# One level of Strassen for the hidden product of six of nine tiles: seven half-block products in place of eight

## The chip, the cores and the metric

The kernel runs on one core of a Trainium2 chip. A core has TensorE (PE in the profile: matrix products, with its weight loads listed as PEld), VectorE (DVE), ScalarE (ACT), GpSimd (POOL) and SyncE (SP, whose queue issues the transfers), an on-chip memory (SBUF) of 128 partitions, a product memory (PSUM) of eight banks of 512 float32 a partition, and HBM behind the DMA engines. The metric is the device time of one execution in microseconds (us).

## The reference

Attention inside chunks of 64 tokens, then a wide layer with g = h cos h:

```python
q, k, v: (8, 8, 576, 64) float32        # batch, heads, sequence, head size
scores = scale * q_c @ k_c.T            # per chunk of 64 tokens
attn = softmax(scores)                  # max subtracted, sum + 1e-9
x = (attn @ v_c) laid out as (4608, 512)
h = x @ w_in                            # (4608, 512) @ (512, 2048)
g = h * np.cos(h)
out = g @ w_out                         # (4608, 2048) @ (2048, 512)
```

The weights arrive as 64-bit floats and are joined to float32 on the chip.

## The kernel before, in words

The 4608 tokens are nine tiles of 512 (t = 0 to 8); the 2048 hidden columns are 16 blocks of 128 (fc). Every float32 factor of the two large products is kept as a rounded high part and the low rest, and a product is three matmuls: high by high, high by low, low by high.

For one (t, fc), `hidden` (line 485) sums h into one PSUM bank: four chunks of the 512 rows of w_in, three matmuls each, 12 matmuls with 128x128 weights (w_in) over 512 moving columns (x, transposed). `activated` (496) then takes six operations in turns of ACT and DVE: the nearest whole turn (506, ACT), h minus that many turns (507, DVE), the sine (508, ACT), times h (509, DVE), the rounded part g_hi (510, ACT) and the rest g_lo (511, DVE). `project` (528) adds g times w_out into four PSUM banks `acc`, one for each 128 tokens (sub), three matmuls of 512 columns each; `finish` (555) copies a bank out after the tile's last block, on ACT for even sub and DVE for odd, and stores it. h has two PSUM banks in turn (`ps_h`), the two attention banks `a0` and `a1` are separate. All matmuls go through line 196, so the trace tells them apart by their tiles.

The first two tiles and the splitting of the weights run in an order that a planner works out (`placed`, `in_order`); it isn't touched. From the third tile on (line 872) the order is written out: for each (t, fc) the product h, the projection of the block three before it (`LAG`), then the six operations. Between them attention for the next tile is threaded in: at fc = 0 a burst of score matmuls (64x64) into the h banks and `a0`, `a1`; row maxima and differences on DVE; at fc = 2 the exponentials on ACT, which need another function table than the sine (ACT_TABLE_LOAD); row sums, quotients and 32 transposes of 32x256 on DVE, spread over the steps by the queue `soon`; at fc = 12 a second burst, weights times v, whose result is split into the high and low parts of x. `take` issues the next entries of a queue; `kept` holds each engine to program order. Loads go through SyncE's queue in program order as well.

The weights stay in SBUF: `w_in` and `w_out`, 16 rooms each, high and low parts side by side (`w_parts`). GpSimd works only in the first stage.

Of the kernel before, what the change touches and what calls it, by code (L numbers as in the profile page):

```python
# [21 lines left out]
P = 128  # L22
# [10 lines left out]

SCORES = 0
WEIGHTED = 12

# [125 lines left out]
def attention_then_cos_ffn(ctx: ExitStack, tc, qT, kT, v, w_in, w_out, out, wide):  # L162
# [51 lines left out]
    w_parts = {}  # L214

# [18 lines left out]
    def split_weight(name, fc, low):  # L234
# [34 lines left out]
        def high():  # L269
            o = SHIFT if name == "in" else 0  # L270
            parts = wts.tile([P, 2 * n + PAD], F32R, name=f"w_{name}{fc}")
            hi, lo = parts[:, o : o + n], parts[:, o + n : o + 2 * n]
            kept(nc.scalar.copy(out=hi, in_=w()))  # L273
            w_parts[name, fc] = (hi, lo)

# [70 lines left out]
    def scores(t, g, banks):  # L346

        for j in range(2):  # L350
            qt, kt = queries.pop((t, 2 * g + j))
            for c in range(NCH):
                pr, par = divmod(c, 2)
                cs, ps = slice(c * CH, (c + 1) * CH), slice(par * CH, (par + 1) * CH)
                o = (j * NPR + pr) * CH
                for h in range(2):
                    hs = slice(h * CH, (h + 1) * CH)
                    matmul(
                        banks[h][ps, o : o + CH], qt[hs, cs], kt[hs, cs], start=True, stop=True
                    )  # L360
        e = weights_of(t, g).rearrange("p a (r h) k -> p a r h k", h=2)
        found = []
        for h in range(2):
            sv = banks[h].rearrange("p (a r k) -> p a r k", a=2, k=CH)
            m = att.tile([P, 2, NPR], F32, name="m", bufs=4)

            def largest(m=m, sv=sv):
                kept(nc.vector.tensor_reduce(out=m, in_=sv, op=ALU.max, axis=AX.X))

            def below(m=m, sv=sv, h=h):  # L370
                mb = m.unsqueeze(3).broadcast_to([P, 2, NPR, CH])
                kept(nc.vector.tensor_tensor(e[:, :, :, h], sv, mb, op=ALU.subtract))

            found.extend((largest, below))
# [64 lines left out]
    def weighted(t, hps, banks):  # L439
# [4 lines left out]
        for j, hp in enumerate(hps):  # L444
            pts = probs.pop((t, hp))
            vt = values.pop((t, hp))
            for pr in range(NPR):
                for par in range(2):
                    ks = slice(par * CH, (par + 1) * CH)
                    o = (j * NPR + pr) * CH  # L450
                    for h in range(2):
# [4 lines left out]
                            start=True, stop=True,  # L456
                        )
        if (t, g) not in x_parts:
# [55 lines left out]
    def activate(t, fc, h):  # L514
# [10 lines left out]
        for queue in (full, soon, late):  # L525
            take(queue, len(queue))

    def project(s):
        t, fc = order[s]
        first = s == 0 or order[s - 1][0] != t  # L530
        last = s == len(order) - 1 or order[s + 1][0] != t
        g_hi, g_lo = g_parts.pop((t, fc))
        w_hi, w_lo = w_parts["out", fc]
        sums_out = []
        for sub in range(NSUB):
# [3 lines left out]
            ss = slice(sub * P, (sub + 1) * P)  # L539

            n = DM // 2 if s == len(order) - 1 and sub == NSUB - 1 else DM
            for a in range(0, DM, n):
                cs = slice(a, a + n)
                matmul(o[:, cs], g_hi[:, ss], w_hi[:, cs], start=first, stop=False)
                matmul(o[:, cs], g_hi[:, ss], w_lo[:, cs], start=False, stop=False)
                matmul(o[:, cs], g_lo[:, ss], w_hi[:, cs], start=False, stop=last and a + n == DM)
                if last:
                    sums_out.append(lambda sub=sub, o=o, cs=cs: finish(t, sub, o, fc == NFC - 1, cs))
        return sums_out
# [5 lines left out]
    def finish(t, sub, o, whole, cs):  # L555
        r0 = t * TOK + sub * P
        to = out[r0 : r0 + P, cs]
# [5 lines left out]
        elif t < NT - 1:  # L563
            os = out_room(sub)
        else:
            if sub % 2 == 0:
                acc["last"] = x_room(t + 1, F32)
            os = acc["last"][:, sub % 2, cs]
        o = o[:, cs]
# [8 lines left out]
    def resume():  # L578

        for sub in range(NSUB):  # L580
            os = acc["partial", sub] = out_room(sub)
            nc.sync.dma_start(out=os, in_=partial[sub])

# [20 lines left out]
    def burst(t, step):  # L604
# [3 lines left out]
        if step == SCORES:  # L608
# [3 lines left out]
        late.extend(first[:2] + second[:2] + first[2:] + second[2:])  # L612

    def prefetch(t):
        for hp in range(HP):
            load_qk(t, hp)
        for hp in range(2):
            load_v(t, hp)
# [71 lines left out]
    def early(t):  # L690
        s, e, z, q, w, p = {}, {}, {}, {}, {}, {}
        for hp in range(HP):
# [10 lines left out]
            e[hp] = piece(ACT, 0.6, lambda hp=hp: exponentials(t, hp), banks_free[which], table=AF.Exp)  # L703
# [169 lines left out]
    for s in range(STAGE, len(order) + LAG):  # L873
        if s < len(order):
            t, fc = order[s]
            h = hidden(t, fc)
            if t + 1 < NT:
                attend(t + 1, fc)
            if fc == WEIGHTED + 1 and t + 2 < NT:
                prefetch(t + 2)  # L880
# [3 lines left out]
        if s < len(order) and t + 1 < NT and fc in (SCORES, WEIGHTED):  # L884
            burst(t + 1, fc)
            through += 1
            full.extend(project(through))
        if s < len(order):
            activate(t, fc, h)
            if t + 1 < NT and fc == 2:  # L890
                exponentials(t + 1)
        take(full, len(full))

# [53 lines left out]
```

## Time and profile before

| | |
|---|---|
| median of 3 runs | 854.6 us (854.23 to 854.71) |
| the profiled execution | 854.07 us, of which its span 852.3 us |
| PE busy | 839.6 us, 99% of the span, 5795 matmuls |
| DVE busy | 554.1 us, 65% |
| ACT busy | 389.3 us, 46% |
| POOL busy | 6.8 us, 1% |
| DMA | 57.52 MB, mean 67 GB/s |
| granted TensorE clock | 0.998 of full speed |

The span is the part of the execution that the trace covers, from the first to the last instruction; the execution's own time lies 1.8 us above it. PE's busy time is the union of its matmuls, which overlap each other at their ends: their distance from start to start is what a matmul costs in a row of them.

### The profile page before, as it was taken

The numbers are of one execution on the slowest core, as the hardware profiler recorded it, in microseconds if no ns is written. First come the engines' busy times: TensorE is split into PE (matmuls) and PEld (weight loads), VectorE is DVE, ScalarE is ACT, GpSimd is POOL, SyncE is SP. The second block draws the span as 40 slices with busy tenths as digits, with TensorE's granted clock in tenths as the row PEclk, the third lists the DMA queues.
The fourth block names the chain that finished last, engine by engine and source line by source line (L and its number), as shares of the span: only waits on it lengthen the run. The fifth ranks groups of instructions, "written<-read, shape, count | busy, mean of one in ns | idle before, by whom it ended". The sixth has DMA issues, their size and how long they took to land.

```text
span 852.3 us, 14049 instructions
## 1 busy us (share of the span) xinstructions
PE 839.6 (99%) x5795; PEld 694.5 (81%) x5795; DVE 554.1 (65%) x942; ACT 389.3 (46%) x637; POOL 6.8 (1%) x12
## 2 busy tenths in 40 slices
PE   6999999999999999999999999999999999999998
PEld 5878888888888888888888888888888888888886
DVE  6978888744786458755775568646974577544332
ACT  4999973333433344342533353335333353333332
POOL 1010000000000000000000000000000000000000
PEclk9999999999999999999999999999999999999999
DMA  9990200420300211020302030022002020001001
GB/s 342 415 412 18 75 1 1 149 99 1 121 4 0 76 62 64 0 75 2 123 1 75 1 125 1 1 75 98 28 0 75 2 75 0 2 1 50 1 1 49
DMA packets 26704, 57.52 MB, mean 67 GB/s; under 512 B 2961, under 2 KB 3217, under 8 KB 26641
## 3 DMA queue, kind: packets, MB, share of 16 engines
q1 hardware_dynamic: 26640, 56.63, 18.3%
q8 instruction: 45, 0.74, 0.4%
q14 instruction: 19, 0.15, 0.1%
HBM read 46.14 MB, written 10.49 MB: 66 GB/s over the span
## 4 chain that ended last, share of the span: by engine, by line
PE 93%; ACT 4%; DVE 1%; DMA 1%; issue 0%; POOL 0%; SPq 0%; ACTq 0%; POOLq 0%
PE h L196 47%; PE acc L196 45%; PE a L196 2%; ACT half L265 1%; DMA kt<-in_kT_dram 1%; ACT w L263 0%; ACT x L469 0%; ACT w_out L273 0%; ACT L381 0%; ACT g_hi L510 0%; ACT g L508 0%; ACT e L381 0%; DVE x L472 0%; ACT w_in L273 0%; POOL e L401 0%
## 5 line engine op out<-in xcount | busy, mean ns | idle before, releaser
L196 PE MATMUL h<-x,w_in 128*128 128x512 f32 x1728 | 413.9, 390 | 0.2 <-DVE g L509 0.2
L196 PEld LDWEIGHTS h<-x,w_in 128*128 128x128 f32 x1728 | 323.8, 188 | 67.9 <-DVE g L509 0.6
L196 PE MATMUL acc<-w_out,g_hi 128*128 128x512 f32 x1154 | 356.9, 390 | 0.0
L196 PEld LDWEIGHTS acc<-w_out,g_hi 128*128 128x128 f32 x1154 | 215.3, 188 | 45.1
L196 PE MATMUL acc<-w_out,g_lo 128*128 128x512 f32 x577 | 224.4, 389 | 0.0
L507 DVE SCALAR_TENSOR_TENSOR g<-g,h 128x512 f32<-128x512 int32 x144 | 98.5, 684 | 141.3 <-ACT g L506 140.3
L506 ACT ACTIVATE g<-h 128x512 int32<-128x512 f32 x144 | 85.9, 597 | 198.8 <-PE h L196 198.6
L508 ACT ACTIVATE g<-g 128x512 f32<-128x512 f32 x144 | 91.1, 633 | 132.1 <-DVE g L507 132.0
L511 DVE TENSOR_TENSOR g_lo<-g,g_hi 128x512 fp32r<-128x512 f32 x144 | 99.6, 691 | 62.1 <-ACT g_hi L510 59.4
L509 DVE TENSOR_TENSOR g<-h,g 128x512 f32<-128x512 f32 x144 | 99.5, 691 | 61.4 <-ACT g L508 59.4
L510 ACT CAST g_hi<-g 128x512 fp32r<-128x512 f32 x144 | 89.5, 621 | 104.6 <-DVE g L509 96.5
L196 PEld LDWEIGHTS acc<-w_out,g_lo 128*128 128x128 f32 x577 | 108.3, 188 | 22.6
L431 DVE STREAM_TRANSPOSE pts<-e 32x256 f32<-32x256 f32 x128 | 55.5, 435 | 2.0
L431 DVE STREAM_TRANSPOSE e<-e 32x256 f32<-32x256 f32 x96 | 41.8, 435 | 1.8
L391 DVE TENSOR_REDUCE z<-e 128x8 f32<-128x512 f32 x36 | 23.8, 678 | 3.7 <-ACT e L381 3.7
L381 ACT ACTIVATE e<-e 128x1024 f32<-128x1024 f32 (+1 forms) x22 | 19.1, 898 | 9.7 <-DVE e L342 9.6
L258 DVE SCALAR_TENSOR_TENSOR w<-w,half 128x512 uint32<-128x512 uint32 x32 | 21.7, 686 | 1.5 <-ACT w L263 0.9
L401 DVE TENSOR_TENSOR e<-e,z 128x512 f32<-128x512 f32 x30 | 20.3, 683 | 0.0
L196 PE MATMUL a<-kt,qt 64*64 64x64 f32 x640 | 19.2, 220 | 0.6 <-DVE x L472 0.6
L196 PEld LDWEIGHTS a<-kt,qt 64*64 64x64 f32 x640 | 17.7, 135 | 2.1 <-issue 1.4
L472 DVE TENSOR_TENSOR x<-a,x 128x512 fp32r<-128x512 f32 (+1 forms) x24 | 14.4, 639 | 0.6 <-ACT x L469 0.5
L196 PEld LDWEIGHTS h<-kt,qt 64*64 64x64 f32 x384 | 11.7, 135 | 2.1 <-issue 2.1
(63 smaller groups left out, 335.1 us busy)
## 6 DMA issues: line engine op xcount, KB each, us to landing
qt<-in_qT_dram SPq DMA_DIRECT2D x36, 256.0 KB, 4.6
kt<-in_kT_dram SPq DMA_DIRECT2D x36, 256.0 KB, 4.9
w_in<-in_w_in_dram SPq DMA_DIRECT2D x16, 512.0 KB, 9.7
w_out<-in_w_out_dram SPq DMA_DIRECT2D x16, 512.0 KB, 9.9
vt<-in_v_dram SPq DMA_DIRECT2D x22, 256.0 KB, 5.2
out_dram<-w SPq DMA_DIRECT2D x16, 256.0 KB, 2.2
out_dram<-half SPq DMA_DIRECT2D x16, 256.0 KB, 2.1
qt<-in_v_dram SPq DMA_DIRECT2D x12, 256.0 KB, 3.0
```

Source lines behind the costliest of these rows:

```text
L196: kept(nc.tensor.matmul(*args, **kw))
L258: kept(nc.vector.scalar_tensor_tensor(bits, bits, 3, low, op0=ALU.logical_shift_left, op1=ALU.bitwise_or))
L381: kept(nc.scalar.activation(e, e, AF.Exp, scale=SCALE))
L391: kept(nc.vector.tensor_reduce(out=sums_of(t)[:, hp], in_=weights_of(t, hp // 2)[:, hp % 2], op=ALU.add, axis=AX.X))
L401: kept(eng.tensor_tensor(e, e, zb, op=ALU.mult))
L431: kept(nc.vector.transpose(out=dst[o : o + BL, :, qb], in_=src[i : i + BL, :, kb]))
L506: lambda: kept(nc.scalar.activation(n, h, AF.Identity, bias=0.25, scale=0.5 / math.pi)),
L507: lambda: kept(nc.vector.scalar_tensor_tensor(g, n, -2.0 * math.pi, h, op0=turns, op1=over)),
L508: lambda: kept(nc.scalar.activation(g, g, AF.Sin, bias=0.5 * math.pi)),
L509: lambda: kept(nc.vector.tensor_tensor(g, h, g, op=ALU.mult)),
L510: lambda: kept(nc.scalar.copy(out=g_hi, in_=g)),
L511: lambda: kept(nc.vector.tensor_tensor(g_lo, g, g_hi.bitcast(F32), op=ALU.subtract)),
```

## The change

Tiles 3 to 8 take h two blocks at a time (a pair k, blocks 2k and 2k+1), with the 512 tokens, the 512 rows of w_in and the two blocks each cut in two. In place of eight products of quarter size there are seven (Winograd's form), each of 256 moving columns and two chunks of 128 rows, in the order A11, S3, S2, A12, A22, S1, S4. The sums between products are made in PSUM: a and d are the halves of one bank, b and c of another; ACT copies a into b and b into c, and later products add onto the copies. d goes to SBUF (`ds`), and DVE adds it to c and b to make the second block h2.

The seven combinations of w_in for each pair are made on GpSimd during tile 2 (`combine`), in the rooms of w_in itself, stored to HBM (`combos`) and streamed back two combinations (512 KB) at a time for every pair of every tile from 3 on (`load_two`), through eight of the freed rooms. The combinations of x are made for each tile by `halves` (11 items for `soon`: four differences on DVE, seven rounded parts on ACT, seven low parts on DVE), from an x that the second burst leaves whole in SBUF. The last-block split of the final copy is dropped. The first burst runs ahead of pair 0 (pair 1 in tile 3), the exponentials in the pair after it, the second burst after pair 5. Projections are cut into parts of one sub (`due_parts`), and `after` says how many of them stand behind the products A11, A22, S1 and S4.

```diff
+LAST_TURN = 5
+FAST = 3
+STREAM = 5
+ROOMS = 8
...
@@ weighted
+        if t >= FAST:
+            x = weights_of(t, g).rearrange("p a (r c) q -> p a r c q", c=2)
+            def taken_out(par):
+                xq = banks[par].rearrange("p (a r q) -> p a r q", a=n, q=CH)
+                kept(nc.scalar.copy(out=x[:, :, :, par], in_=xq))
+            return [lambda: taken_out(0), lambda: taken_out(1)]
...
@@ finish
-        elif sub % 2 == 0 or cs.start:
+        elif sub % 2 == (t == NT - 1):
             kept(nc.scalar.copy(out=os, in_=o))
...
+    HALF = TOK // 2
+    NPAIR = NFC // 2
+    A11, S3, S2, A12, A22, S1, S4 = range(7)
+    combos = [hbm.tile([P, 2, 2, HALF], F32, name=f"combo{m}") for m in range(7 * NPAIR // 2)]
...
+    def combine(k):
+        one, two = in_halves(k)
+        for j, a in ((A11, one[:, :, 0]), (A12, one[:, :, 1]), (A22, two[:, :, 1])):
+            store(combo(k, j), a)
+        def pool(out, a, b, op):
+            kept(nc.gpsimd.tensor_tensor(out, a, b, op=op))
+        w1, w2 = (dec.tile([P, 2, HALF], F32, name="w") for _ in range(2))
+        for w, a in ((w1, one), (w2, two)):
+            pool(w, a[:, 0].bitcast(F32), a[:, 1].bitcast(F32), ALU.add)
+        u, v = (wts.tile([P, 2, HALF], F32, name=f"half{i}") for i in range(2))
+        pool(u[:, 0], w2[:, 0], w2[:, 1], ALU.add)
+        pool(u[:, 1], w1[:, 0], w2[:, 0], ALU.subtract)
+        pool(v[:, 0], u[:, 0], w1[:, 0], ALU.subtract)
+        pool(v[:, 1], w1[:, 1], v[:, 0], ALU.subtract)
+        for s, room in ((u[:, 0], two[:, :, 0]), (u[:, 1], one[:, :, 0]), (v[:, 0], one[:, :, 1]), (v[:, 1], two[:, :, 1])):
+            kept(nc.gpsimd.tensor_copy(room[:, 0], s))
+            pool(room[:, 1], s, room[:, 0].bitcast(F32), ALU.subtract)
+    def keep_sums(k):
+        one, two = in_halves(k)
+        for j, a in ((S1, two[:, :, 0]), (S2, one[:, :, 1]), (S3, one[:, :, 0]), (S4, two[:, :, 1])):
+            store(combo(k, j), a)
+        for fc in (2 * k, 2 * k + 1):
+            if STREAM <= fc < STREAM + ROOMS:
+                load_two(fc - STREAM)
+    def load_two(i):
+        if i < (NT - FAST) * len(combos):
+            room = w_in_room(STREAM + i % ROOMS, F32R)[:, SHIFT : SHIFT + 2 * TOK]
+            load(room.bitcast(F32), combos[i % len(combos)].rearrange("p n h d -> p (n h d)"))
...
+    def halves(t):
...
+        return [
+            lambda: (begin(), difference(S1, "pts", x(0, 1), x(0, 0)), high(A11)),
+            lambda: (difference(S3, "vt", x(1, 1), x(0, 1)), high(S1)),
+            lambda: (difference(S2, "pts", x(1, 1), of(S1)), high(S3)),
+            lambda: (difference(A22, "vt", x(1, 0), of(S2)), high(S2)),
+            lambda: (low(A11), high(A12)),
+            lambda: (low(S3), high(A22)),
+            lambda: (low(S2), high(S4)),
+            lambda: low(A12), lambda: low(A22), lambda: low(S1), lambda: low(S4),
+        ]
+    def go(n):
+        for _ in range(min(n, len(due_parts))):
+            take(full, len(full))
+            due_parts.popleft()()
+    def pair(t, k):
+        behind = bool(exponentials_due)
+        if behind:
+            after = (4, 0, 2, 2)
+        elif len(due_parts) < 12:
+            after = (1, 0, 2, 1) if k > LAST_TURN else (1, 0, 1, 2)
+        elif t == NT - 1 and k == NPAIR - 1:
+            after = (2, 1, 2, 0)
+        else:
+            after = (3, 0, 2, 3)
+        bank1, bank2 = (ps_h.tile([P, TOK], F32, name="h") for _ in range(2))
+        a, d = bank1[:, :HALF], bank1[:, HALF:]
+        b, c = bank2[:, :HALF], bank2[:, HALF:]
...
+            for cc in range(2):
+                w_hi, w_lo = w[:, 0, cc], w[:, 1, cc]
+                x_hi, x_lo = x[:, 0, cc], x[:, 1, cc]
+                matmul(out, w_hi, x_hi, start=begin and cc == 0, stop=False, skip_group_check=True)
+                matmul(out, w_hi, x_lo, start=False, stop=False, skip_group_check=True)
+                matmul(out, w_lo, x_hi, start=False, stop=cc == 1, skip_group_check=True)
+            if n % 2:
+                load_two(n // 2 + ROOMS)
...
+        product(a, A11, begin=True)
+        take(exponentials_due, 1)
+        copy(b, a)
+        take(exponentials_due, 1)
+        take(pair_before, len(pair_before))
+        quota = [-(-len(soon) // (LAST_TURN + 1 - k if k <= LAST_TURN else NPAIR - k))]
+        if behind:
+            quota = [4]
...
+        go(after[0])
+        take(full, len(full))
+        product(d, S3)
+        product(b, S2)
+        copy(c, b)
+        product(a, A12)
+        copy(ds, d)
+        product(c, A22)
+        whole(g1[:, first], a)
+        some(0 if behind else 3)
+        turn(g1[:, first], a)
+        sine(g1[:, first])
+        go(after[1])
+        product(b, S1)
+        add(h2[:, first], c)
+        add(h2[:, second], b)
+        times(g1[:, first], a)
+        go(after[2])
+        whole(g2, h2)
+        some(1)
+        turn(g2, h2)
+        some(1)
+        product(b, S4)
+        go(after[3])
+        whole(g1[:, second], b)
+        turn(g1[:, second], b)
+        sine(g1[:, second])
+        sine(g2)
+        some(1)
+        times(g1[:, second], b)
+        times(g2, h2)
+        pair_before.extend([
+            lambda: high(g1, 2 * k), lambda: low(g1, 2 * k),
+            lambda: high(g2, 2 * k + 1), lambda: low(g2, 2 * k + 1),
+        ])
+        if k <= LAST_TURN:
+            some(quota[0])
+        else:
+            pair_before.append(lambda: some(quota[0]))
...
+    def run_of_short(t, scored):
+        take(pair_before, len(pair_before))
+        burst(t, scored)
+        take(late, len(late))
+        go(NSUB)
...
+            soon.extend(halves(t))
...
+        for k in range(NPAIR):
+            if max(2 * k + 1, 3) == fc:
+                combine(k)
+            if max(2 * k + 1, 3) == fc - 2:
+                keep_sums(k)
...
+    for t in range(FAST, NT):
+        for k in range(NPAIR):
+            if t + 1 < NT and k == (t == FAST):
+                run_of_short(t + 1, True)
+                pair(t, k)
+                exponentials_due.extend([lambda t=t: exponentials(t + 1, 0), lambda t=t: weights_from(t + 1)])
+            else:
+                pair(t, k)
+            if t == FAST and k == 0:
+                keep_sums(NPAIR - 1)
+            if t + 1 < NT and k == LAST_TURN:
+                run_of_short(t + 1, False)
```

`whole`, `turn`, `sine`, `times`, `high` and `low` inside `pair` are the six operations of `activated`, for g1 (block 2k, in two halves of 256 tokens) and g2 (block 2k+1). `some(n)` takes up to n entries of `soon`, within the pair's quota. `weights_from` issues the second half of the exponentials and puts the 41 attention items (row sums, quotients, transposes) into `soon`. In tile 2 a step now takes at most four items of `soon` at its end, where it took all.

## Rows read from the trace of the kernel before

**Rows 1.** The page, busy time: us, share of the span, instructions.
```profile
PE 839.6 (99%) x5795; PEld 694.5 (81%) x5795; DVE 554.1 (65%) x942; ACT 389.3 (46%) x637; POOL 6.8 (1%) x12
```

**Rows 2.** Windows: busy us (instructions) of each engine; clock, DMA share, GB/s.
```profile
588.00:676.00 88.00, 88.00 (x626) 72.91 (x625) 58.51 (x102) 34.95 (x55) 0.00 (x0) 1.00 0.14 49
```

**Rows 3.** Timeline 589 to 612: start, us, engine, line, operation; idle before.
```profile
589.80 0.62 ACT L510 CAST g_hi<-g 128x512 fp32r<-128x512 f32 x1 [0.34 <-DVE g L509]
590.33 0.58 ACT L573 COPY w<-acc 128x512 f32<-128x512 f32 x1
...
590.93 1.28 ACT L381 ACT_TABLE_LOAD   x1
...
592.22 2.01 ACT L381 ACTIVATE e<-e 128x1024 f32<-128x1024 f32 x2
...
603.90 1.77 DVE L431 STREAM_TRANSPOSE pts<-e 32x256 f32<-32x256 f32 x4
...
605.70 0.69 DVE L507 SCALAR_TENSOR_TENSOR g<-g,h 128x512 f32<-128x512 int32 x1
606.30 0.69 DVE L401 TENSOR_TENSOR e<-e,z 128x512 f32<-128x512 f32 x1
```

**Rows 4.** Timeline of ACT, 670 to 700.
```profile
682.47 1.28 ACT L381 ACT_TABLE_LOAD   x1
```

**Rows 5.** Timeline 655 to 672: PE hands a block to ACT and DVE.
```profile
656.35 2.88 PE L196 MATMUL h<-x,w_in 128*128 128x512 f32 x12
...
659.07 0.62 PE L196 MATMUL acc<-w_out,g_hi 128*128 128x512 f32 x2
...
659.33 0.60 ACT L506 ACTIVATE g<-h 128x512 int32<-128x512 f32 x1 [1.37 <-PE h L196]
...
659.96 0.69 DVE L507 SCALAR_TENSOR_TENSOR g<-g,h 128x512 f32<-128x512 int32 x1 [1.28 <-ACT g L506]
...
661.79 2.88 PE L196 MATMUL h<-x,w_in 128*128 128x512 f32 x12
```

**Rows 6.** Timeline 845 to the end: six matmuls of 256 columns.
```profile
847.86 0.40 PE L196 MATMUL acc<-w_out,g_hi 128*128 128x256 f32 x2
...
848.09 0.28 PE L196 MATMUL acc<-w_out,g_lo 128*128 128x256 f32 x1
848.09 0.31 PEld L196 LDWEIGHTS acc<-w_out,g_hi 128*128 128x128 f32 x2
...
848.45 0.28 PE L196 MATMUL acc<-w_out,g_lo 128*128 128x256 f32 x1
848.76 0.42 DVE L575 COPY x<-acc 128x256 f32<-128x256 f32 x1 [0.70 <-PE acc L196]
```

**Rows 7.** Groups by line and shape: busy us, mean ns; idle before, releaser.
```profile
L508 ACT ACTIVATE g<-g 128x512 f32<-128x512 f32 x144 | 91.1, 633 | 132.1 <-DVE g L507 132.0
...
L401 POOL TENSOR_TENSOR e<-e,z 128x512 f32<-128x512 f32 x6 | 6.1, 1044 | 52.3 <-DVE z L396 52.3
...
L472 DVE TENSOR_TENSOR x<-a,x 128x256 fp32r<-128x256 f32 x4 | 1.5, 420 | 0.1
L469 ACT CAST x<-acc 128x256 fp32r<-128x256 f32 x4 | 1.4, 372 | 0.0
```

**Rows 8.** Timeline 12 to 24: attention of the first tile.
```profile
15.15 0.57 ACT L416 COPY pts<-h 128x512 f32<-128x512 f32 x1
...
15.78 1.20 PE L196 MATMUL acc<-pts,vt 64*64 64x64 f32 x31
...
18.20 0.68 DVE L401 TENSOR_TENSOR e<-e,z 128x512 f32<-128x512 f32 x1
18.29 0.64 ACT L469 CAST x<-a 128x256 fp32r<-128x256 f32 x2
...
18.97 0.76 DVE L472 TENSOR_TENSOR x<-a,x 128x256 fp32r<-128x256 f32 x2
...
19.03 0.63 PE L410 MATMUL h<-ident,e 128*128 128x128 f32 x4 [0.17 <-DVE e L401]
```

**Rows 9.** Timeline of PE: the first product of tiles 2 and 3.
```profile
204.06 2.88 PE L196 MATMUL h<-x,w_in 128*128 128x512 f32 x12
...
295.60 2.88 PE L196 MATMUL h<-x,w_in 128*128 128x512 f32 x12
```

**Rows 10.** The page, GB/s that the DMA engines moved in 40 slices.
```profile
GB/s 342 415 412 18 75 1 1 149 99 1 121 4 0 76 62 64 0 75 2 123 1 75 1 125 1 1 75 98 28 0 75 2 75 0 2 1 50 1 1 49
```

More of the change, by code (lines that the diff above doesn't have):

```diff
@@ L524, in activate, with projected_by_parts @@
         rest()
-        for queue in (full, soon, late):
-            take(queue, len(queue))
+        take(full, len(full))
+        take(soon, most)
+        take(late, len(late))
     def project(s):
+        sums_out = []
+        for run in projected_by_parts(s, sums_out):
+            run()
+        return sums_out
+    def projected_by_parts(s, sums_out):
         t, fc = order[s]
@@ L531, in project, with part @@
         last = s == len(order) - 1 or order[s + 1][0] != t
[L532 to L535, printed above, removed]
+        def part(sub):
+            g_hi, g_lo = g_parts[t, fc]
+            w_hi, w_lo = w_parts["out", fc]
             if first:
@@ L539, in project, with finish @@
             ss = slice(sub * P, (sub + 1) * P)
[L541 to L549, printed above, removed]
+            matmul(o, g_hi[:, ss], w_hi, start=first, stop=False)
+            matmul(o, g_hi[:, ss], w_lo, start=False, stop=False)
+            matmul(o, g_lo[:, ss], w_hi, start=False, stop=last)
+            if last:
+                sums_out.append(lambda sub=sub, o=o: finish(t, sub, o, fc == NFC - 1))
+        return [lambda sub=sub: part(sub) for sub in range(NSUB)]
     def out_room(sub):
         return (wts if sub % 2 else dec).tile([P, DM], F32, name=f"half{sub // 2}" if sub % 2 else "w")
-    def finish(t, sub, o, whole, cs):
+    def finish(t, sub, o, whole):
         r0 = t * TOK + sub * P
-        to = out[r0 : r0 + P, cs]
+        to = out[r0 : r0 + P, :]
         if not whole:
@@ new lines, in run_of_short, with weights_from, begin @@
+    def run_of_short(t, scored):
+        take(pair_before, len(pair_before))
+        burst(t, scored)
+        take(late, len(late))
+        go(NSUB)
+        if scored:
+            for hp in range(2):
+                load_v(t, hp)
+        else:
+            soon.extend(halves(t))
+            if t + 1 < NT:
+                prefetch(t + 1)
+    def weights_from(t):
+        exponentials(t, 1)
+        for hp in range(2, HP):
+            load_v(t, hp)
+        soon.extend(lambda hp=hp: total(t, hp) for hp in range(HP))
+        soon.append(lambda: inverse(t))
+        for hp in range(2):
+            soon.append(lambda hp=hp: quotient(t, hp))
+        for hp in range(HP):
+            def begin(hp=hp):
+                pieces["turn"] = turned(t, hp)
+                pieces["turn"][0]()
+            soon.append(begin)
+            soon.extend(lambda i=i: pieces["turn"][i]() for i in range(1, 8))
+            if hp < 2:
+                soon.append(lambda hp=hp: quotient(t, hp + 2))
@@ L611, in burst @@
             first, second = (weighted(t, (2 * g, 2 * g + 1), banks[g]) for g in range(2))
[L612 removed]
+        n = len(first) // 2
+        late.extend(first[:n] + second[:n] + first[n:] + second[n:])
     def prefetch(t):
@@ L702, in early @@
             banks_free[which] = piece(DVE, 0.6, rest_of(key, 1), m, room)
-            e[hp] = piece(ACT, 0.6, lambda hp=hp: exponentials(t, hp), banks_free[which], table=AF.Exp)
+            e[hp] = piece(ACT, 0.6, lambda hp=hp: exponentials_early(t, hp), banks_free[which], table=AF.Exp)
         for hp in range(HP):
@@ L872, in attention_then_cos_ffn @@
     through = STAGE - 1 - LAG
[L873 to L880, printed above, removed]
+    for s in range(STAGE, STAGE + NFC):
+        t, fc = order[s]
+        h = hidden(t, fc)
+        attend(t + 1, fc)
+        if fc == WEIGHTED + 1:
+            soon.extend(halves(t + 1))
+            prefetch(t + 2)
         if s - LAG > through:
```

133 lines of the change are left out of this document (113 added, 20 removed).

## The prediction

> **What bounds the kernel now.** I read the page's shares first. TensorE (PE) is busy for 99% of the span and VectorE (DVE) for 65% [rows 1]; the reader is to see that only PE's instruction count, or a hole torn into its stream, moves the end. Then a late tile by windows: PE 88.00 of 88, DVE 58.5, ScalarE (ACT) 35 [rows 2]. A tile with attention for the next one takes 91.54 us, from the exponentials' table load of one tile to that of the next [rows 3, 4]. One pair of product (h) and projection (acc), 24 matmuls of 512 columns, takes 661.79 - 656.35 = 5.44 us, so 0.2267 a matmul [rows 5]. Sixteen make 87.04; the remaining 4.5 are two attention bursts of 2.25.
>
> The one place with 256-column matmuls is the tail: five steps from 847.86 to 848.45, 0.118 each [rows 6]. Half of 0.2267 would be 0.113: cutting a matmul in two costs some 5 ns a piece.
>
> **What the change takes from PE.** Two neighbouring blocks of h were 24 matmuls of 512, 5.44 us. They become 7 products of 6 matmuls of 256: 42 x 0.118 = 4.96 (a product 0.71). That is 0.484 a pair of blocks; 8 pairs in 6 tiles are 48, so **23.2 us** less PE work (0.1176 to 0.119 a step is what the rounding of the rows allows: 21.2 to 24.0). Projections (a "part" is 3 matmuls, 0.68), bursts and the first three tiles keep their PE work.
>
> By the Trainium skill (TensorE: Matmul & The Clock Gate, section Back-to-back issue gap) a warm matmul steps by N/2.4 + 2.5 ns, which makes 0.109 and 0.216 and an estimate of 28 us saved; the rows carry some 10 ns more per matmul, and the measured steps stand.
>
> **What it adds elsewhere.** A pair now costs ACT three PSUM copies of 256 columns, two roundings and two sines of 256, the same of 512, and two casts: about 5.2 us, 42 a tile, plus 7 casts of x; with the rest about 51 of some 90. On DVE six operations of 256 (0.42) and four of 512 (0.69) make 5.3, 42 a tile; attention keeps about 25 of the 58.5, and the differences and low parts of x bring 7.6 where 2.7 were: some 73 of 90 [rows 2, 3, 7]; a sine of 256 is taken as 0.42, the 0.63 of 512 less the 0.21 by which ACT's 256 copy (0.37) is shorter than its 512 copy (0.58). Neither is a bound by its sum. But both run in program order, PE now waits for them inside a pair, and at the places below the order puts much work ahead of what PE needs.
>
> The prices for a walk of these queues. Independent operations start closer than their length: on ACT a 0.62 cast is followed after 0.53, two of 256 take 0.64, two exponentials 2.01 (so steps of 0.53, 0.27, 0.96); on DVE 0.60 after a 0.69, and 0.34 for a 256 (two in 0.76); transposes 0.44 [rows 3, 8]. A dependent one pays the full length and 0.03 (659.93 to 659.96) [rows 5]. From PE's last matmul slot to a copy 0.20 [rows 6], to the rounding 0.26 [rows 5]. ACT to PE 0.06 (15.72 to 15.78), DVE to PE 0.15 (18.88 to 19.03) [rows 8]. A bank is handed over whole: the copy of the left half at 848.76 began 0.03 after the last matmul into the right half [rows 6], so a product into one half waits for a reader of the other. An ACT copy from PSUM into PSUM has no row; I take the 0.37 of PSUM into SBUF [rows 7], with 0.27 (its step) and 0.74 (twice) as bounds.
>
> *Ordinary pair* (parts 3, 0, 2, 3 between the products). The copy of b into c needs 0.20 + 0.37 + 0.06 = 0.63 and hides under the A12 product (0.71). At 0.74 it would miss by 0.29, 14 us over 48 pairs. The copy of a into b hides under three parts. The S4 product waits for the two adds, which end 0.96 after S1, under two parts (1.36). No stall.
>
> *One part before S4* (pair 0 of tiles 3 to 7, pair 1 of tile 3). From S1's end: add c at 0.20, add b 0.54 to 0.96, plus 0.15 makes 1.11 against 0.68: 0.43, six times, **2.6**.
>
> *Pair with the exponentials* (pair 1 of tiles 4 to 7). ACT ends pair 0's last sine 0.70 after this pair's start. Then the table load to 1.98, an exponential to 2.94, the copy into b to 3.21, the second exponential to 4.17, two casts and two copies of finished sums to 6.29; only then the copy into c, 6.66, PE at 6.72. PE arrives there after 0.71 + 4 x 0.68 + 3 x 0.71 = 5.56. Stall 1.16, four times, **4.6**. In tile 3 the finished sums come a pair earlier: 0.1.
>
> *The second burst* (after pair 5). From S4's end: turn to 1.09, one transpose, both sines (ACT, to 2.06), the last times 2.09 to 2.78, three transposes to 4.02, PE at 4.17. The burst's last quarter, which reads them, would begin after 3 parts and three quarters at 3.82: 0.35, four times, 1.4. Tile 3 has its exponentials a pair later and squeezes the same items into three pairs, 12 or 13 each; six transposes are left behind pair 5's last times: 1.7. Together **3.1**.
>
> *Pair 7.* In pair 6 six casts of x stand in ACT's order, three of them ahead of the first sine. From pair 6's start: rounding 4.00, casts to 5.87, sine to 6.28, its times on DVE, one difference, turn of the second block from 7.24, a low part, turn 8.44, sines 8.89 and 9.20, sixth cast 9.74, pair 7's copy into b 10.27 to 10.64, PE 10.70. PE is there at 7.69 + 0.71 + 2.04 = 10.44: 0.26, five times, **1.3**.
>
> *Tile 2 and the stream.* The combinations run on GpSimd, which is otherwise idle: per pair two operations of 512 (1.04 [rows 7]) and twelve of 256 (between half of that and all of it: 8.3 to 14.6). I take 8.9, nearer to half; 71 us from the fourth step of tile 2 (204.06 + 3 x 5.44 = 220) to 291, before tile 3 begins at 295.6 [rows 9]. Each pair writes 1.8 MB to HBM; from tile 3 on 28 loads of 512 KB a tile, 14.7 MB in 88 us, 167 GB/s where the queue has shown 342 to 415 [rows 10]. Eight rooms are 16 products, over two pairs or 20 us, ahead: cost nothing while GpSimd is on time. The last copy (512 on ACT for 256 on DVE and 256 on ACT in sequence) gains 0.2 and its larger store gives it back.
>
> Sum: 2.6 + 4.6 + 0.1 + 3.1 + 1.3 = 11.7 of new waiting, 23.2 - 11.7 = 11.5 less. The profiled execution took 854.07 (852.3 of span), 0.5 under the median 854.6: **842.6**.
>
> **Rivals.**
> *The queues eat the gain (slower).* If back-to-back operations cost their whole length in these chains (0.62 and 0.69 for 0.53 and 0.60), the same walk gives: 0.5 six times; 1.8 in pair 1; 0.9 at the burst, and in tile 3 3.4 with the pairs before it; 1.9 in pair 7, since the wait for the copy grows to 1.4 and S4's to 0.5: about 5.1 a tile in tiles 4 to 7, 7 in tile 3, 27.5 in all: 858.4. It decides above 23 us of stalls, 4.6 a tile with attention. For it: each chain crosses three engines, and DVE is at 80%. Against: the rows show the shorter steps.
> *No stalls.* If the order catches up everywhere, 831. For it: all stalls but pair 1's are under 0.5; against: pair 1's does not hang on a close race.
> *GpSimd late.* With 256 columns at 1.04 a pair's combinations take 14.6, the last end at 337, 41 us into tile 3. SyncE's queue stands behind them with the loads, and product 22, due some 33 us into the tile, waits about 10 us: 852. The trace has GpSimd at work only in the first stage [rows 7]. By the Trainium skill (SBUF — State Buffer, section Who interferes with whom) a DVE operation with two SBUF inputs and a reading GpSimd operation block each other; tile 2 has some 31 such, an estimate of up to 21 us more for GpSimd, most of which the 20 us ahead absorb. No run here shows it yet.
> *Weight loads no longer hide.* A load's record is 0.19, longer than a 256-column step. Were that the step, a pair would be 42 x 0.19 = 7.98, 2.54 more than before, 122 us in all: 976. Against: two loads in the tail fill 0.31 together and their matmuls come 0.118 apart [rows 6], though only six in a row. The Trainium skill (TensorE: Matmul & The Clock Gate, section The mechanism) says a load overlaps running matmuls only in other row groups; these use all rows and overlap, so the trace disagrees.
>
> **Chances.** Forecast (836 to 849) 0.50; queues eat the gain (850 to 866) 0.26, of which 0.05 still faster and 0.04 within 0.2%; no stalls (829 to 835) 0.14; GpSimd late 0.07, mostly faster still; loads 0.03. A measurement of this kernel tells 0.2% (1.7 us) from nothing. Faster 0.50 + 0.14 + 0.05 + 0.06 = 0.75, same 0.05, slower 0.20. The range, 831 to 859, takes in the dear end of the walks and the cheap end of the step; the forecast's own is 836 to 849.
>
> **What would show it.** Right: 256-column h matmuls 0.118 apart; in tile 8 no idle PE and a pair (7 products and 8 parts) in 10.4; in tiles 4 to 7 PE idle some 2.2 us a tile, the longest piece in pair 1 ahead of an A22 product with ACT's copy as releaser; a tile in about 90 us. Wrong: idle PE ahead of every A22 (the PSUM copy is dearer), PE waiting for DMA or GpSimd's stores in tile 3, a step above 0.125, DVE over 85% in tiles 3 to 7 with PE waiting for DVE before S4 in ordinary pairs, or a third tile that grows.

## The result, and the profile after

The changed kernel takes 858.16 us (median of 7 runs, 855.84 to 858.35), the kernel before 854.23 beside it: ratio 1.0042 [1.003, 1.0054], slower by 0.4%. The forecast said 842.6 and faster with 0.75: its sign was wrong. The time lies in its range only because the range reached to a rival at 858.4, and that rival's mechanism is not what the trace shows: that part is luck.

The page of the changed kernel, busy time and granted clock in 40 slices [rows 1]:

```profile
PE 828.3 (97%) x6656; PEld 716.2 (84%) x6656; DVE 632.7 (74%) x1176; ACT 464.9 (54%) x918; POOL 98.0 (11%) x124
...
PEclk9999999999999989999999999999999999999999
```

PE is busy for 11.3 us less than before, in a span 4.1 longer (856.4 for 852.3), so it now stands idle some 28 us where it stood 13. (Its work fell by more, as shown below: a slower stretch, and the ends of records that reach into a hole, count as busy.) The one 8 in the clock is the 15th slice, 300 to 321 us. Windows there, and of a whole later tile (columns as in [rows 2]):

```profile
295.00:305.00 10.00, 4.46 (x23) 3.33 (x21) 8.57 (x11) 3.27 (x6) 9.60 (x11) 0.90 0.96 342
305.00:315.00 10.00, 9.80 (x104) 8.77 (x108) 4.04 (x9) 3.75 (x9) 7.27 (x12) 0.76 0.66 218
...
411.00:502.00 91.00, 89.48 (x786) 79.41 (x786) 71.56 (x144) 49.36 (x106) 0.00 (x0) 1.00 0.63 208
```

Tile 3 begins at 297.67. In the first window PE is busy for 4.46 us of 10, DVE for 8.57 and GpSimd for 9.60; in the second the clock is down. The later tile has its full clock, and PE is idle for 1.5 of 91.

**An ordinary pair does what was forecast.** PE's timeline in tile 8, from one A11 product to the next [rows 5, 6]:

```profile
771.42 0.86 PE L208 MATMUL h<-x,w_in 128*128 128x256 f32 x6
772.12 2.23 PE L208 MATMUL acc<-w_out,w_in 128*128 128x512 f32 x9
774.19 2.27 PE L208 MATMUL h<-x,w_in 128*128 128x256 f32 x18
776.30 1.58 PE L208 MATMUL h<-w_in,w_in 128*128 128x256 f32 x12
777.72 0.86 PE L208 MATMUL acc<-w_out,w_in 128*128 128x512 f32 x3
...
779.11 0.88 PE L208 MATMUL h<-w_in,w_in 128*128 128x256 f32 x6
...
781.87 0.86 PE L208 MATMUL h<-x,w_in 128*128 128x256 f32 x6
```

Start to start, 18 products take 2.11 (0.117 each) and 12 take 1.42 (0.118). The eight parts between them take 10.45 less 4.94, 5.51, where 24 matmuls in a row took 5.44. A pair is 10.45 for 10.88: 0.43 saved, 20.6 over 48 pairs.

**Tiles 4 to 7.** Table load to table load, as [rows 3, 4]:

```profile
502.09 1.28 ACT L401 ACT_TABLE_LOAD   x1
...
592.97 1.28 ACT L401 ACT_TABLE_LOAD   x1
```

That is 90.88 for 91.54, where eight pairs alone would give 91.54 - 3.44 = 88.10: 2.8 of waiting a tile. The waits of PE by the view of waits (what waited, for what: us in total, times, longest):

```profile
PE h L208 <- ACT h L783: 8.9, 5, 5.5
...
PE a L208 <- DVE e L451: 3.5, 5, 1.5
...
PE h L208 <- DVE e L388: 1.3, 1, 1.3
...
PE h L208 <- DVE w_in L786: 1.0, 6, 0.2
```

L783 is ACT's copy from PSUM, L451 DVE's transposes, L388 its differences behind the first burst, L786 the adds. Five waits for ACT's copy: four of 0.85, one in each of tiles 4 to 7 ahead of the A22 product, and one of 5.5. Five waits of the second burst for the transposes: four of 0.5, one of 1.5 in tile 3. Six waits of 0.16 for the adds ahead of S4. One of 1.3 in tile 3 for the differences. This view counts from the end of a record; the hole in PE's stream, from start to start, is 0.16 longer.

**Tile 3.** The wait of 5.5, in the timeline of PE, DVE, ACT and GpSimd:

```profile
282.74 0.40 POOL L658 CAST w_in<-half 128x256 fp32r<-128x256 f32 x1 [1.69 <-DMA combo<-w_in]
...
284.95 0.69 DVE L536 SCALAR_TENSOR_TENSOR g<-g,h 128x512 f32<-128x512 int32 x1 [6.47 <-ACT g L535]
...
288.45 1.77 DVE L540 TENSOR_TENSOR g_lo<-g,g_hi 128x512 fp32r<-128x512 f32 x1
...
297.66 0.59 ACT L535 ACTIVATE g<-h 128x512 int32<-128x512 f32 x1
297.67 0.86 PE L208 MATMUL h<-x,w_in 128*128 128x256 f32 x6
...
298.79 1.22 DVE L718 TENSOR_TENSOR w_in<-vt,w_in 128x512 fp32r<-128x512 f32 x1
...
298.92 0.49 PE L208 MATMUL acc<-w_out,g_lo 128*128 128x512 f32 x1
299.40 0.86 POOL L658 CAST w_in<-half 128x256 fp32r<-128x256 f32 x1
...
300.73 1.21 DVE L718 TENSOR_TENSOR w_in<-e,w_in 128x512 fp32r<-128x512 f32 x1
...
301.86 0.67 DVE L536 SCALAR_TENSOR_TENSOR g<-g,h 128x512 f32<-128x512 int32 x1
302.57 0.63 ACT L537 ACTIVATE g<-g 128x512 f32<-128x512 f32 x1 [4.32 <-DVE g L536]
...
304.54 0.37 ACT L783 COPY h<-h 128x256 f32<-128x256 f32 x1
...
304.95 4.21 PE L208 MATMUL h<-x,w_in 128*128 128x256 f32 x18 [5.54 <-ACT h L783]
308.96 1.96 PE L208 MATMUL h<-w_in,w_in 128*128 128x256 f32 x12
```

Read it from the end. PE waits for the copy of a into b. The copy stands in ACT's program order behind the sine (302.57) and the cast of block 15, the last of tile 2; the sine waits 4.32 for that block's turn on DVE. The turn waits for nothing but its place: ACT had its input ready at 298.25, DVE comes to it at 301.86, after the low parts of x for tile 3 (L718), back to back at 1.2 us each. [rows 3] and [rows 8] have DVE operations of this size at 0.68 to 0.69. They are stretched, and the groups of DVE between 284 and 306 show which:

```profile
L540 DVE TENSOR_TENSOR g_lo<-g,g_hi 128x512 fp32r<-128x512 f32 x3 | 3.6, 1208 | 0.7 <-ACT g_hi L539 0.7
...
L538 DVE TENSOR_TENSOR g<-h,g 128x512 f32<-128x512 f32 x3 | 2.0, 682 | 0.7 <-ACT g L537 0.7
L536 DVE SCALAR_TENSOR_TENSOR g<-g,h 128x512 f32<-128x512 int32 x3 | 2.0, 679 | 6.5 <-ACT g L535 6.5
...
L718 DVE TENSOR_TENSOR x<-e,x 128x512 fp32r<-128x512 f32 x2 | 2.3, 1162 | 0.0
```

Turn (L536) and times (L538) take one operand, h, from PSUM: 0.68. The low parts (L540, L718) take both from SBUF: 1.16 to 1.21 on average. The Trainium skill (SBUF — State Buffer, section Who interferes with whom) says that a DVE operation with two SBUF inputs and a GpSimd operation that reads SBUF block each other, and that one with at most one SBUF input, outside the modes that use two ports, does not; the trace agrees, on both sides of the line. GpSimd pays too: a cast of 0.40 while DVE stands idle (282.74) is 0.86 beside the low parts (299.40).

After the hole PE starts at the lower of its two clock levels: 18 products from 304.95 to 308.96 are 0.223 each, 1.2 GHz for 2.4. The 30 up to 310.76 take 5.81 for 3.53, 2.3 more. Tile 3's holes sum to 11.1 (5.7 and 1.44 in its first two pairs, 1.65 and 0.33 in the second burst, 0.35 and 0.30 ahead of S4, small ones); with the clock 13.4. Counted by the starts of the tiles' first products (297.67 and 402.29) it is a little more: 104.6 us, 14.3 above eight pairs and the three bursts in them (8 x 10.45 and 3 x 2.25).

The account: -20.6 (pairs) + 14.3 (tile 3) + 4 x 2.8 (tiles 4 to 7) + 0 (tile 8) - 0.7 (the stages before tile 3) = +4.2; the spans differ by 4.1. The last term: tile 3 starts at 297.67 and not at 295.60 [rows 9], but 12 more projection matmuls, 2.7 us, lie ahead of it.

### The profile page after: what moved, and what is told of

Read it like the earlier page. It is cut to its first block, busy times and chain, and to the rows that moved or that the text cites. A ratio compares the mean times of both kernels' runs of the same rounds, so it can differ in the third digit from the quotient of the medians.

```text
span 856.4 us, 16912 instructions
## 1 busy us (share of the span) xinstructions
PE 828.3 (97%) x6656; PEld 716.2 (84%) x6656; DVE 632.7 (74%) x1176; ACT 464.9 (54%) x918; POOL 98.0 (11%) x124
## 4 chain that ended last, share of the span: by engine, by line
PE 78%; DVE 8%; ACT 8%; DMA 2%; issue 2%; SPq 1%; DVEq 0%; ACTq 0%
PE h L208 39%; PE acc L208 38%; DVE e L451 2%; DVE g L795 1%; ACT g L799 1%; DMA qt<-in_qT_dram 1%; PE a L208 1%; DVE w_in L786 1%; DMA w_in<-in_w_in_dram 1%; DVE g L802 1%; ACT half L278 1%; DVE g_lo L810 1%; ACT L401 1%; ACT e L401 1%; ACT w L276 1%
## 5 line engine op out<-in xcount | busy, mean ns | idle before, releaser
L208 PE MATMUL h<-x,w_in 128*128 128x256 f32 (+1 forms) x1728 | 292.8, 319 | 7.0 <-ACT h L783 5.5
L208 PE MATMUL acc<-w_out,g_hi 128*128 128x512 f32 x960 | 299.3, 393 | 0.0
L208 PEld LDWEIGHTS h<-x,w_in 128*128 128x128 f32 x1728 | 256.7, 189 | 41.4 <-ACT h L783 10.2
L208 PE MATMUL h<-w_in,w_in 128*128 128x256 f32 x864 | 119.9, 282 | 4.4 <-ACT h L783 3.4
L208 PEld LDWEIGHTS h<-w_in,w_in 128*128 128x128 f32 x864 | 111.7, 188 | 12.2 <-DVE w_in L786 4.5
L783 ACT COPY h<-h 128x256 f32<-128x256 f32 x96 | 34.5, 359 | 122.9 <-PE h L208 114.3
L799 ACT ACTIVATE g<-g 128x256 f32<-128x256 f32 x144 | 65.2, 484 | 52.1 <-DVE g L795 52.1
L208 PE MATMUL acc<-w_out,w_in 128*128 128x512 f32 x288 | 73.6, 393 | 0.0
L451 DVE STREAM_TRANSPOSE pts<-e 32x256 f32<-32x256 f32 x128 | 55.5, 434 | 2.2
L536 DVE SCALAR_TENSOR_TENSOR g<-g,h 128x512 f32<-128x512 int32 x48 | 32.8, 683 | 30.9 <-ACT g L535 30.5
L535 ACT ACTIVATE g<-h 128x512 int32<-128x512 f32 x48 | 28.7, 597 | 42.0 <-PE h L208 41.9
L537 ACT ACTIVATE g<-g 128x512 f32<-128x512 f32 x48 | 30.4, 634 | 38.2 <-DVE g L536 38.1
L540 DVE TENSOR_TENSOR g_lo<-g,g_hi 128x512 fp32r<-128x512 f32 x48 | 38.3, 799 | 14.8 <-ACT g_hi L539 14.0
L802 DVE TENSOR_TENSOR g<-h,g 128x256 f32<-128x256 f32 x96 | 40.3, 420 | 11.7 <-ACT g L799 11.0
L786 DVE TENSOR_TENSOR w_in<-h,w_in 128x256 f32<-128x256 f32 x96 | 36.3, 420 | 13.5 <-PE h L208 13.5
```

The source lines that it names most:

```text
L208: kept(nc.tensor.matmul(*args, **kw))
L451: kept(nc.vector.transpose(out=dst[o : o + BL, :, qb], in_=src[i : i + BL, :, kb]))
L536: lambda: kept(nc.vector.scalar_tensor_tensor(g, n, -2.0 * math.pi, h, op0=turns, op1=over)),
L537: lambda: kept(nc.scalar.activation(g, g, AF.Sin, bias=0.5 * math.pi)),
L540: lambda: kept(nc.vector.tensor_tensor(g_lo, g, g_hi.bitcast(F32), op=ALU.subtract)),
L783: kept(nc.scalar.copy(out=out, in_=in_))
```

## Experiments

Ratios are against the kernel before, run on the same chips (854.14, 853.94 and 854.05 us in the three sets).

One execution of each kernel was traced, and the first wait of tile 3 differs between executions of code that is the same up to there: 5.5 (changed kernel) and 3.9 (casts later); 2.0, 1.0 and 1.6 (x halves earlier, both, five items); 1.4, 0.3 and 1.6 (GpSimd earlier on top of both, all four edits, one step too far). A step of 1.5 between two traces shows nothing there.

**Without GpSimd's arithmetic.** The kernel keeps the stores and the stream, and leaves out the sums.

```diff
-        def pool(out, a, b, op):
-            kept(nc.gpsimd.tensor_tensor(out, a, b, op=op))
...
-            kept(nc.gpsimd.tensor_copy(room[:, 0], s))
-            pool(room[:, 1], s, room[:, 0].bitcast(F32), ALU.subtract)
```

> Leaves out GpSimd's arithmetic on w_in in tile 2 (the stores and loads of all seven combinations stay, with uncombined contents). Theory (GpSimd holds up DVE's operations with two SBUF inputs, so that the last two blocks of tile 2 and the x halves finish late and PE stands still in the first pair of tile 3, 5.7 us, then runs 2.3 us longer at the lower clock, then waits 1.4 in pair 1): DVE's L540 and L718 back at 0.69, the first pair without a gap over 1 us, 848 (846 to 850). Rival (the x halves standing ahead of the last blocks' turn in DVE's order are enough by themselves): the gap stays at 3 us or more, 853 or more. Rival (the stream of combinations through SyncE is late): 857 to 859.

851.77 us, 0.9971 [0.9959, 0.9982]: faster than before, 6.4 under the changed kernel. DVE's groups of the same stretch, the first product after the copy, and a window:

```profile
L540 DVE TENSOR_TENSOR g_lo<-g,g_hi 128x512 fp32r<-128x512 f32 x3 | 2.1, 693 | 1.0 <-ACT g_hi L539 0.7
L538 DVE TENSOR_TENSOR g<-h,g 128x512 f32<-128x512 f32 x3 | 2.1, 692 | 0.9 <-ACT g L537 0.7
...
L703 DVE TENSOR_TENSOR x<-e,x 128x512 fp32r<-128x512 f32 x2 | 1.4, 683 | 0.0
```

```profile
299.47 2.42 PE L208 MATMUL h<-x,w_in 128*128 128x256 f32 x18 [0.36 <-ACT h L768]
```

```profile
305.00:315.00 10.00, 9.46 (x169) 7.75 (x168) 9.11 (x16) 4.07 (x8) 0.00 (x0) 1.00 0.90 305
```

The low parts are 0.68 to 0.69 again, the wait of 5.54 is 0.36, and the clock stays up there. So the hole is GpSimd's arithmetic beside DVE's, not a long queue by itself. Tile 3 takes 97.7 us by its starts, for 104.6. It was 4 short of the expectation all the same: tile 3 keeps 5.5 us of holes, and behind the second burst, in which PE waits 1.5, the lower clock comes after all:

```profile
367.30:371.00 3.70, 3.70 (x12) 2.91 (x11) 2.52 (x5) 2.05 (x4) 0.00 (x0) 0.55 0.72 244
```

Seven matmuls of 512 columns take 0.427 each there, for 0.2267: 1.4 us, with the one before them 1.5. In the changed kernel the same hole of the burst is followed by the full rate.

**The x halves one block earlier**, so that their low parts end before block 15's turn.

```diff
-        if fc == WEIGHTED + 1:
-            soon.extend(halves(t + 1))
...
         activate(t, fc, h, 4)
+        if fc == WEIGHTED:
+            soon.extend(halves(t + 1))
+            take(soon, 6)
```

> The x halves of tile 3 are issued one block earlier, six of the eleven right behind the second burst, where DVE stood idle for 6.5 us; GpSimd works as before. Theory (lateness of DVE at the end of tile 2, by GpSimd and by the order together): the 5.7 us gap and the lower clock behind it go, the 1.4 us in pair 1 may stay, 850 (848 to 852). Rival (stream of combinations late): no change, 857 to 859.

854.25 us, 1.0005 [0.9994, 1.0017], 3.9 better than the changed kernel but 4 short. Two rows of PE:

```profile
302.68 3.91 PE L208 MATMUL h<-x,w_in 128*128 128x256 f32 x18 [2.00 <-ACT h L783]
...
325.84 0.94 PE L208 MATMUL h<-x,w_in 128*128 128x256 f32 x6 [1.38 <-DMA w_in<-combo]
```

The first wait falls from 5.54 to 2.00, but the 18 products behind it still take 3.91, at the lower clock. The 1.3 of the next pair is gone; it is gone as well from the trace of the next experiment, which changes nothing ahead of it, so that is not shown to be this edit's doing. And PE, which comes 4.8 earlier to the first product of pair 2 (324.3 for 329.0), now waits there for the stream. GpSimd ends at 331 and not 326, not for the low parts beside it, since its work took 101.4 for 100.4, but since it began at 229.6 and not at 226.1 (227.7 and 228.8 in two more traces with this order; why is open). The two engines take turns at being late.

**The casts later.** In the pair with the exponentials the casts and low parts of the pair before go behind the copy into c.

```diff
-        take(pair_before, len(pair_before))
+        if not behind:
+            take(pair_before, len(pair_before))
...
         copy(c, b)
+        if behind:
+            take(pair_before, len(pair_before))
```

> In the pair with the exponentials the casts and low parts of the pair before stand behind the copy into c, not ahead of it. Theory (ACT's order holds PE ahead of A22, 1.0 us in each of four tiles): these gaps shrink to 0.1, 854 (853 to 855). Rival (the wait moves to the parts behind S1, which need the casts): within 0.5 us of the changed kernel, 858.

854.26 us, 1.0002 [0.9992, 1.0011]: 3.9 better than the changed kernel, as expected. The A22 product of tile 5 in the changed kernel, then here:

```profile
508.02 1.70 PE L208 MATMUL h<-w_in,w_in 128*128 128x256 f32 x12 [0.85 <-ACT h L783]
```

```profile
503.22 1.66 PE L208 MATMUL h<-w_in,w_in 128*128 128x256 f32 x12
```

The hole of 1.0 is gone. Tiles 4 to 7 take 89.9, 89.9, 89.9 and 84.9 us by their starts, for 90.9, 90.9, 90.9 and 85.9, and four times 1.0 is the gain: this term of the prediction was right in place, cause and size.

**Both**, the two edits above together.

> Both edits together. If they are independent, the sum of both: 846 (844 to 848), faster than both kernels. If the early x only moves the lateness into the first pairs: 850 or more.

851.44 us, 0.9959 [0.9945, 0.9973]; 5 short, and the same trade as with the halves alone. The traced execution took 849.03:

```profile
300.70 2.42 PE L208 MATMUL h<-x,w_in 128*128 128x256 f32 x18 [1.01 <-ACT h L783]
...
323.17 0.94 PE L208 MATMUL h<-x,w_in 128*128 128x256 f32 x6 [2.14 <-DMA w_in<-combo]
...
329.40 1.64 PE L208 MATMUL h<-w_in,w_in 128*128 128x256 f32 x12 [0.43 <-DMA w_in<-combo]
```

**GpSimd starts earlier.** On top of both, the sums of the first five pairs go into other rooms, so that they need not wait for the last split of the weights.

```diff
+        if k < 5:
+            r1, r2 = (xp.tile([P, 2, TOK], F32, name="x0") for _ in range(2))
+            w1, w2 = (r1[:, i].rearrange("p (d n) -> p d n", d=2) for i in range(2))
...
+            u, v = (r2[:, i].rearrange("p (d n) -> p d n", d=2) for i in range(2))
...
-if max(2 * k + 1, 3) == fc:
+if 2 * k + 1 == fc:
```

> Both edits of before (early x, casts later), and GpSimd's combinations of the first five pairs use rooms of the third tile's x, free since the tile before, so that they start at the second step of tile 2 (some 212) where they waited for stores until 228. Theory (GpSimd's end, 327, sets the loads of combinations that PE waited for, 2.3 and 0.6 us in tile 3): GpSimd ends near 310, no wait of PE for a load, 848.5 (847 to 850). Rival (the wait was the queue's length, not GpSimd's end): the load waits stay, 851.

848.06 us, 0.9934 [0.9913, 0.9954]. GpSimd works from 200 to 315 and no product waits for the stream any more; the first wait of tile 3, 1.39, is where it was.

**Five items for three** of attention ahead of the first turn in the pairs up to the second burst (on top of both, without the rooms).

```diff
-        some(0 if behind else 3)
+        some(0 if behind else 5 if k <= LAST_TURN else 3)
```

> Both edits of before, and in pairs 0 to 5 five attention items instead of three stand ahead of the first turn, where DVE waits for ACT, so that two fewer are left for the end of a pair. Theory (the second burst waits for transposes left behind pair 5): its wait falls from 0.7 to 0.1 in tiles 4 to 7 and from 2.0 to about 1 in tile 3, 848 (847 to 850). Rival (the turn becomes late and S4 waits instead): 851 or more.

849.22 us, 0.9949 [0.9933, 0.9965]. The second burst's hole of 0.67 is gone in tiles 4 to 7; in tile 3 1.66 becomes 1.26. In each of tiles 4 to 7 one hole of 0.38 to 0.46 ahead of S4 comes new, as the rival had it, though smaller. By their starts tiles 4 to 7 are only 0.2 to 0.3 shorter each, so of the 2.2 gained some 1.5 are placed.

**All four edits**, the full computation.

> All four edits. If their gains add: 845 (843.5 to 847). If they share one wait: 848.

846.53 us (845.49 to 848.0), 0.9915 [0.99, 0.993]: faster than both kernels. Its waits of PE in tiles 3 to 8, from the view of waits:

```profile
PE h L208 <- DVE w_in L793: 2.6, 12, 0.3
...
PE a L208 <- DVE e L451: 1.1, 1, 1.1
PE h L208 <- DVE e L388: 0.5, 1, 0.5
PE h L208 <- ACT h L790: 0.3, 1, 0.3
```

What stays is mostly the adds ahead of S4, 0.2 each. This trace has both cases of DVE's low parts side by side: GpSimd waits for a store from 281.8 to 284.6, and the four operations with two SBUF inputs that DVE starts between 282.2 and 284.2 take 0.68 to 0.69; the three from 288.9, with GpSimd at work again, take 1.22, 1.78 and 1.78.

**The same without GpSimd's arithmetic**, to see what it still costs; the sums are left out as above.

> All four edits, and GpSimd's arithmetic on w_in left out (stores and loads stay). It shows what GpSimd still costs in the version with all edits: 843 if only the gap at the start of tile 3 (1 us) is left of it; 845, as that version, if nothing is.

844.53 us, 0.9887 [0.9871, 0.9904]: 2.0 less. A new hole of 1.4 at 311 is put down to "issue". A hole of this kind stands behind the first burst of tile 3 in two more traces: 0.7 in the first experiment, 1.7 in the next one. In all three a transfer of the instruction queue (0.02 MB) ends within 0.7 us of the moment at which PE stops; most such transfers are followed by no hole, so the cause stays open.

**GpSimd's earlier start alone**, on the changed kernel. If the end of GpSimd's work were what counts, this would help; if it is the time both engines spend side by side, little would change.

> The change with GpSimd's earlier start alone (its end near 313, not 326); x halves and casts as changed. Theory (what counts is that GpSimd runs beside the x halves, from 285 to 303, not when it ends): the gap in the first pair of tile 3 stays at 3 to 6 us with the lower clock behind it, only the 1.4 in pair 1 goes, 856 (854.5 to 857.5). Rival (GpSimd's late end is the cause): the gap falls under 1 us, 848 to 851.

857.15 us, 1.0034 [1.0023, 1.0046], within the expected range.

```profile
304.32 2.07 PE L208 MATMUL h<-x,w_in 128*128 128x256 f32 x8 [4.05 <-ACT h L790]
```

GpSimd ends 10 us earlier, at 316, but it still works beside the low parts of x, and the wait stays at 4.05 (5.5 and 3.9 in the two traces without this edit). The 1.3 of pair 1 is gone, as said beforehand, but the hole of 1.7 put down to "issue" stands in its place. The same earlier start was worth 3.4 by the medians on top of the earlier halves, where it took away the wait for the stream.

**One step too far.** On all four edits, the copies of finished sums go behind the copy into c, and the short pairs give S4 one part more.

```diff
-            after = (1, 0, 2, 1) if k > LAST_TURN else (1, 0, 1, 2)
+            after = (1, 0, 2, 1)
...
         if behind:
+            take(full, len(full))
             take(pair_before, len(pair_before))
```

> The version with all four edits; in addition the copies of finished sums in the pair with the exponentials stand behind the copy into c, and the short pairs have one part less at their end and one more ahead of S4. Theory (S4 waits 0.3 in each short pair for the adds, for want of a second part): these gaps go, no new one ahead of A22, 844.5 (843 to 846). Rival (the wait returns ahead of A22, since the pair with the exponentials now begins earlier against ACT): 846.5, as the version with all four.

851.45 us, 0.9975 [0.9964, 0.9985]: 5 us slower than without, where some 2 less were expected. Around tile 5:

```profile
498.52 2.38 PE L208 MATMUL h<-x,w_in 128*128 128x256 f32 x18 [0.38 <-ACT h L790]
504.48 0.97 PE L208 MATMUL h<-w_in,w_in 128*128 128x256 f32 x6 [0.40 <-DVE w_in L793]
514.82 0.98 PE L208 MATMUL h<-w_in,w_in 128*128 128x256 f32 x6 [0.31 <-DVE w_in L793]
```

In this stretch all four edits had two waits ahead of S4, of 0.16 in pair 0 and 0.19 in pair 2. The first is gone, as the theory had it; the second is 0.31, one of 0.40 in pair 1 comes new, and another, ahead of it, waits for the copy of a into b. Tile 5 takes 90.9 by its starts for 89.7, and four such tiles make nearly all of the 5 us. Which of the two edits does which was not taken apart.

## Why the prediction was wrong, by its own steps

**What the change takes from PE: right in kind, 2.6 too high.** The step of a 256-column product is 0.117 to 0.118, as taken from six matmuls of the tail [rows 6]. The term that was mis-sized is the parts: eight between short products take 5.51, not 5.44, so 20.6 is saved for 23.2. (The formula of the Trainium skill that the prediction set beside its step is given on that page, TensorE: Matmul & The Clock Gate, section Back-to-back issue gap, as that of an isolated matmul; the forecast does not use it.)

**ACT's copy from PSUM to PSUM: right.** 0.37 was taken, 0.36 measured at the rows of L783; no ordinary pair waits for it.

**The walks of the queues: right in place but for pair 7, 2.4 low in sum for tiles 4 to 7.** Measured as holes, against the forecast: one part before S4 0.31 (0.43); the exponentials' pair 1.0 (1.16); the second burst 0.67 (0.35), in tile 3 1.98 (1.7); pair 7 none (0.26). A tile of 4 to 7 loses 2.8 for 2.2, the rest in small holes around the bursts. The experiment with the later casts shows the largest of these by itself.

**"Tile 2 and the stream ... cost nothing while GpSimd is on time": the step that failed.** It asked when GpSimd's results are due and found them early enough, and in the changed kernel no product waits for the stream. That was in part luck: GpSimd ended at 326 and not at 291, and where PE came earlier (x halves earlier, both) it did wait, 1.4 and 2.1. It did not ask what GpSimd does to an engine that runs beside it. The rule on two SBUF inputs was at hand in the prediction itself, and was used for GpSimd's time alone ("an estimate of up to 21 us more for GpSimd"); the same blocking read from DVE's side was never priced, and DVE's queue at the seam of tiles 2 and 3 was never walked. There stand seven low parts of x, with block 14's operations among them, then block 15's turn, and behind the turn, by way of ACT's order, the first copy of the first pair. The 14 operations with two SBUF inputs between 284 and 306 grew by some 6.7 us over those without GpSimd: 3.6 for 2.1 at L540's three, 8.0 for 4.8 at L718's seven, 4.8 for 2.8 at the four differences. PE's first hole is 5.7 with it and 0.5 without, and 2.3 more went by the clock. Tile 3 loses 14.3 for the forecast's 2.9, 11.4 of the 15.6 by which the forecast missed (the parts are 2.6, the walks 2.4, the stages before tile 3 0.7 the other way). Without GpSimd's arithmetic 6.4 come back at once; the rest of tile 3's excess is there without it too.

**GpSimd's price: too low.** A pair of blocks was put at 8.9 and the whole at 71 us; it worked from 226.06 to 326.42, 12.5 a pair:

```profile
226.06 1.29 POOL L647 TENSOR_TENSOR w<-w_in 128x512 f32<-128x512 f32 x1 [166.94 <-DMA out_dram<-half]
...
325.68 0.74 POOL L647 TENSOR_TENSOR w_in<-half,w_in 128x256 fp32r<-128x256 f32 x1
```

Alone, two of 512 at 1.29, eight of 256 at 0.74 and four casts at 0.40 make 10.1. Of the 100.4 us GpSimd was busy for 91.2, where 10.1 a pair would be 80.8, so some 10 are the blocking by DVE; 4.0 are waits for stores and 1.4 one for DVE.

**The rivals.** "The queues eat the gain" named 858.4, within 0.3 of the result, but asked for 5.1 a tile in tiles 4 to 7; they lose 2.8, and the excess sits in tile 3, where it gave 7. Its number was met by another mechanism. "GpSimd late" had the right pair of engines and looked for the damage in the stream; the stream became late only when the experiments let PE come earlier. "Weight loads no longer hide" is refuted by 0.117 a product at 0.19 a load.

**What stays open.** Without GpSimd's arithmetic the terms above (842.6 + 2.6 + 2.4, and 2.6 for the holes left in tile 3) make 850.2, and 851.8 was measured; the lower clock behind the second burst is 1.5 of the 1.6 that are missing. Why the clock falls behind that burst in this trace and in that of the later casts, and not in the changed kernel, where the hole is as long, is open; so is the "issue" hole. All four edits reach 846.53, 3.9 above the forecast: 2.6 are the parts, and the traced execution, 845.49, lies 1.0 under the median. What its tiles lose comes to 12.1 (5.9 in tile 3, 1.6 in each of tiles 4 to 7), about the forecast's 11.7, but in other places.

## What to carry to other kernels

Work given to an idle engine is priced twice: when its result is due, and what it does to the engines that run beside it; for GpSimd that means listing the DVE operations with two SBUF inputs in the same stretch, and walking DVE's queue with them at 1.2 us for 0.69. Walk the seam between the old order and the new one first, since there two queues' backlogs meet. And when a fix for one engine's lateness makes another late, as the earlier halves did here, look for time that lies free before both (GpSimd idle from 200 to 226) rather than for another order.

## What the runs showed of the hardware

- A DVE operation of 512 float32 columns with both inputs in SBUF took 0.88 to 1.77 us beside GpSimd's, 1.2 mostly (changed kernel, 284 to 306), against 0.68 to 0.69 without its arithmetic or while it waited; those with one input in PSUM stayed at 0.68.
- GpSimd alone: 1.29 for a sum of 512 columns, 0.74 of 256, a cast of 256 0.40; beside DVE's work, up to 1.22 for a sum of 256 columns and 0.88 for the cast.
- After 5.7 us without work PE ran 18 products at 0.223 each, against 0.117; the granted clock of that window (305 to 315) was 0.76. Behind a burst with a hole of 1.7 it ran 512-column matmuls at 0.427 for 0.2267 in two traces (without GpSimd's arithmetic, granted clock 0.55 from 367.3 to 371, and with the casts later), and at the full rate in the changed kernel.
- Between 256-column products the 512-column matmuls took 0.2297 each (5.51 for 24), against 0.2267 in a row of them.
